# A planned order on VectorE: scans and reciprocals at their measured durations, half masks and counts at other steps

## The chip, the cores and the metric

One NeuronCore of a Trainium2 chip runs the whole program. Its engines have in-order queues of their own: TensorE (PE, with its weight loads listed as PEld), VectorE (DVE), ScalarE (ACT), GpSimd (POOL), and SyncE (SP), which issues most DMA. Engines wait for one another by semaphores. The metric is the time of one execution on the device, in microseconds (us).

## The reference, cut to what matters

A gated linear attention (4 batches, 8 heads, 768 tokens, head size 48) makes the rows of a mixture of experts with a two-level gate (3072 tokens of 384, 4 groups of 4 experts, hidden size 1024). Each token goes to one expert.

```python
for t in range(S):
    state = alpha[:, :, t, :, None] * state + np.einsum('bhd,bhe->bhde', k[:, :, t], v[:, :, t])
    y[:, :, t] = np.einsum('bhd,bhde->bhe', q[:, :, t], state)
x = np.ascontiguousarray(attn_out.transpose(0, 2, 1, 3)).reshape(B * S, H * D)
...
g_idx = np.argmax(g_logits, axis=1)
...
    e_idx = np.argmax(e_logits, axis=1)
...
        h = np.maximum(xg[mask_e] @ w1[g, e], 0.0)
        ye = h @ w2[g, e]
        out[tok_idx] = combined[:, None] * ye
```

## The kernel before

**The attention stage.** The tokens are cut into 24 chunks of 128 (6 to a batch; chunk n is step n of every series below), the 8 heads lie in 4 pairs over 112 partitions. For one chunk, in words and by the names of the plan:

- SP loads it (`load`, L463). DVE scans the gates backward (`rev`, L469, tile kd), takes the reciprocal of the end values (`turn`, L475, tile starts) and scans forward (`forth`, L480, tile cq).
- POOL multiplies the keys by kd (`key`, L485) and the queries by cq (`query`, L489).
- PE multiplies keys with queries (`score`, L503) into the two PSUM tiles zs, one for each head of a pair. There is one set of zs, so the scores of chunk n + 1 wait until both halves of chunk n are read.
- Each half is masked to the causal triangle and put into the tile sm, in one of two ways: DVE multiplies it by a mask in one step (`mask`, L512), or ACT copies it (`mask`, L517) and POOL cuts it (`cut`, L520).
- PE transposes the keys (`turn_k`, L532, into a part of the zo of the chunk before, after ACT's copy of that zo), ACT copies them (`kept`, L537), PE multiplies them with the values (`gain`, L545), DVE adds the old state (`grow`, L554, tile sums), and ACT scales the sum by kd to the new state (`scale`, L558, four for a chunk).
- PE makes the outputs from sm (L569) and adds what the old state gives (L578), in the PSUM tile zo. ACT copies zo (`copy`, L584, tile yt). PE turns yt into rows of the experts' input and gate logits (`row`, L592), which ACT keeps (L597, L609).

**Routing, by groups of chunks.** Group 0 is chunks 0 to 5, group 1 chunks 6 to 11, and so on. DVE chooses the expert of each token (from `logits`, L612, to `pick`, L673) and its weight (`weigh`). PE counts the tokens ahead of each one with small matmuls (`counts`, L773 to L781), DVE takes out the token's own count (`own`, L720) and makes its place (`place`, L727), and POOL sends each chunk's rows to these places in DRAM with one indirect DMA (`scatter`, L746). After the scatters of groups 0 and 1 SP fetches the first rows of two experts (L802), which DVE transposes (`xt`, L810).

**The experts.** From about 123 us PE multiplies the rows of all 16 experts (L281), ACT applies the relu (L297) and copies (L308), and POOL sends the results to their tokens.

**What sets the order.** Every step of the attention and routing stage is an entry of a plan: a name, an engine, an estimated duration, what it comes after. `Plan.order` (L52) is a list scheduler that runs when the program is built. It plays the plan through with the estimates, and gives each engine, whenever it comes free, the entry with the longest way still to go among those that are ready within `patience` us; `spread` adds a random number from `seed` to each entry's way. What comes out is one fixed order for each engine, and the queues of the chip follow it whatever the durations turn out to be. `BY_VECTOR[n]` says how many of the two mask halves of chunk n DVE does (the rest are ACT's and POOL's), and `COUNTED[g]` at which place in PE's hand-written series of quarter chunks the counts of group g stand.

## Time and profile before

| what | value |
|---|---|
| time, median of 3 runs | 379.44 us (378.81 to 379.56) |
| the profiled execution | 381.04 us |
| its span from the first to the last instruction | 379.2 us |
| mean granted clock of PE | 0.997 |
| busy: PE, PEld | 369.1 us (97%), 350.5 us (92%) |
| busy: DVE, ACT, POOL | 157.5 (42%), 119.5 (32%), 200.8 us (53%) |

The profiled execution's time is 1.84 us longer than its span, and 1.60 us above the median. Busy shares are over the whole span; the attention stage is its first third, and DVE and POOL have most of their work there.

### The profile page before, as it was taken

The page shows a single profiled execution, that of the slowest core. Times are in us where ns is not written, and L with a number is a line of the kernel's source. Part 1 is how long each engine was busy: PE and PEld are TensorE (multiplying, and loading weights), DVE is VectorE, ACT ScalarE, POOL GpSimd, SP SyncE. Part 2 cuts the span into 40 slices and gives each one's busy share as a digit, 9 for nine tenths or more (in the row PEclk, how much of TensorE's full clock was granted, in tenths as well). Part 3 has the DMA queues.
Part 4 walks back from the last instruction along what each step waited for, and adds up shares of the span by engine and source line. Part 5 has one row for each costly group of instructions (what it writes and reads, how often), then busy time and mean ns, then how long its engine had stood idle before and what let it go on. Part 6 is the DMA issues. An engine that isn't in the chain of part 4 may idle for free.

```text
span 379.2 us, 10153 instructions
## 1 busy us (share of the span) xinstructions
PE 369.1 (97%) x4120; PEld 350.5 (92%) x4120; DVE 157.5 (42%) x346; ACT 119.5 (32%) x315; POOL 200.8 (53%) x241
## 2 busy tenths in 40 slices
PE   7899999999999999999999999999999999999994
PEld 5788888888879999999999999999999999999983
DVE  7799899998866420238202022020220211201200
ACT  2666757866653220211112121121211212111210
POOL 6898779999876042616254261634525326236251
PEclk9999999999999999999999999999999999999998
DMA  7999997879873599999976475866769667755001
GB/s 276 397 401 399 409 402 265 267 252 338 329 240 149 165 295 346 344 352 361 339 247 217 183 244 227 285 225 209 235 238 300 218 200 247 284 199 192 8 22 37
DMA packets 30787, 98.08 MB, mean 259 GB/s; under 512 B 18040, under 2 KB 19764, under 8 KB 26131
## 3 DMA queue, kind: packets, MB, share of 16 engines
q1 hardware_dynamic: 25955, 87.87, 66.6%
q0 software_dynamic: 4784, 9.55, 7.3%
q8 instruction: 33, 0.54, 0.6%
q14 instruction: 15, 0.12, 0.1%
HBM read 85.76 MB, written 12.07 MB: 258 GB/s over the span
## 4 chain that ended last, share of the span: by engine, by line
PE 93%; DVE 2%; issue 1%; DMA 1%; ACT 1%; POOL 0%; POOLq 0%; DVEq 0%
PE bank L281 63%; PE zs L503 6%; PE zo L569 6%; PE bank L592 5%; PE zo L578 3%; PE zo L532 3%; PE bank L545 3%; PE zs L281 2%; PE bank L1359 2%; DVE kd L469 1%; DVE cq L480 1%; DMA in<-in_rows_dram 1%; PE bank L781 1%; ACT yt L584 0%; POOL in L489 0%
## 5 line engine op out<-in xcount | busy, mean ns | idle before, releaser
L1194 POOL DMA_INDIRECT out_dram<-yq,dst_q x98 | 95.4, 974 | 146.0 <-DVE yq L1190 109.6
L281 PE MATMUL bank<-hT,w 128*64 128x96 f32 (+14 forms) x768 | 117.5, 318 | 0.0
L281 PEld LDWEIGHTS bank<-hT,w 128*128 128x128 f32 (+1 forms) x768 | 115.5, 183 | 0.0
L281 PE MATMUL bank<-xt_e,w 128*64 128x120 f32 (+14 forms) x816 | 113.5, 311 | 0.0
L281 PEld LDWEIGHTS bank<-xt_e,w 128*128 128x128 f32 (+1 forms) x816 | 111.6, 178 | 0.2 <-issue 0.2
L1237 DVE SCALAR_TENSOR_TENSOR dst_q<-xq,past_q 128x7 int32<-128x7 int32 (+1 forms) x13 | 2.2, 166 | 150.5 <-DMA out_dram<-yq,dst_q 150.5
L297 ACT ACTIVATE hT<-bank 128x192 f32<-128x192 f32 (+15 forms) x68 | 32.0, 471 | 97.7 <-PE bank L281 74.8
L308 ACT COPY yT<-bank 128x192 f32<-128x192 f32 (+28 forms) x30 | 11.9, 396 | 98.5 <-PE bank L281 98.5
L746 POOL DMA_INDIRECT slots_d<-xr,place x24 | 24.1, 1006 | 6.7 <-issue 3.6
L592 PE MATMUL bank<-wr,yt 112*64 112x116 f32 x384 | 25.7, 267 | 0.3 <-ACT yt L584 0.3
L592 PEld LDWEIGHTS bank<-wr,yt 112*64 112x64 f32 x384 | 20.6, 137 | 1.0 <-ACT yt L584 0.5
L1187 DVE STREAM_TRANSPOSE yq<-yT 128x672 f32<-128x672 f32 (+2 forms) x16 | 12.6, 789 | 18.3 <-ACT yT L308 18.3
L485 POOL TENSOR_TENSOR in<-in,kd 112x512 f32<-112x512 f32 (+1 forms) x15 | 16.7, 1118 | 5.9 <-DVE kd L469 5.9
L517 ACT COPY sm<-zs 128x512 f32<-128x512 f32 x27 | 15.8, 588 | 12.2 <-PE zs L503 11.1
L558 ACT ACTIVATE state<-sums,kd 112x48 f32<-112x48 f32 x64 | 17.9, 334 | 3.0 <-DVE sums L554 2.8
L469 DVE TENSOR_TENSOR_SCAN kd<-in,starts 112x516 f32<-112x516 f32 (+1 forms) x15 | 17.0, 1140 | 4.1 <-DMA in<-in_rows_dram 3.1
L489 POOL TENSOR_TENSOR in<-in,cq 112x512 f32<-112x512 f32 (+1 forms) x16 | 16.9, 1058 | 3.4 <-DVE cq L480 3.3
L503 PE MATMUL zs<-in 48*64 48x128 f32 (+1 forms) x352 | 16.2, 274 | 2.3 <-POOL in L489 2.2
L520 POOL TENSOR_SCALAR_AFFINE_SELECT sm<-sm 128x512 f32<-128x512 f32 x27 | 17.0, 641 | 1.6 <-ACT sm L517 1.5
L480 DVE TENSOR_TENSOR_SCAN cq<-in,starts 112x516 f32<-112x516 f32 (+1 forms) x16 | 17.3, 1090 | 1.1
L503 PEld LDWEIGHTS zs<-in 48*64 48x64 f32 (+1 forms) x352 | 13.5, 148 | 4.0 <-POOL in L489 3.2
L584 ACT COPY yt<-zo 112x512 f32<-112x512 f32 x24 | 14.1, 586 | 8.5 <-PE zo L578 6.6
(161 smaller groups left out, 406.0 us busy)
## 6 DMA issues: line engine op xcount, KB each, us to landing
w<-in_w_dram SPq DMA_DIRECT2D x36, 1536.0 KB
in<-in_rows_dram SPq DMA_DIRECT2D x11, 962.5 KB
w<-in_rows_dram SPq DMA_DIRECT2D x10, 962.5 KB
xq<-slots_d SPq DMA_DIRECT2D x28, 85.8 KB
slots_d<-blank SPq DMA_DIRECT2D x2, 980.0 KB
xq<-slots_d SPq DMA_DIRECT2D x24, 73.5 KB
out_dram<-yq,dst_q POOLq DMA_INDIRECT x98
in<-in_rows_dram SPq DMA_DIRECT2D x4, 256.0 KB
```

The costliest lines, as they stand in the source:

```text
L281: nc.tensor.matmul(z[s], lhsT=w[:, s], rhs=x, start=first, stop=last, skip_group_check=True)
L297: nc.scalar.activation(out=hT[:, f0:f0 + 2, 0:n], in_=z[:, 0:2 * n].rearrange("p (f t) -> p f t", f=2), func=AF.Relu)
L469: nc.vector.tensor_tensor_scan(out=flat(c.kd[:, p0:p1])[:, ::-1], data0=c.t[0:R, A1 * p1:A1 * p0:-1], data1=one_col.to_broadcast([R, A1 * ...
L480: nc.vector.tensor_tensor_scan(out=flat(c.cq[:, p0:p1]), data0=c.t[0:R, A1 * p0:A1 * p1], data1=starts[0:R, A1 * p0:A1 * p1], initial=1.0, ...
L489: nc.gpsimd.tensor_tensor(out=c.q[:, p0:p1], in0=c.q[:, p0:p1], in1=c.cq[:, p0:p1, 1:A1], op=ALU.mult)
L503: nc.tensor.matmul(c.zs[i][s, p, :], lhsT=c.k[r, p, s], rhs=c.q[r, p, :], start=True, stop=True)
L520: nc.gpsimd.affine_select(out=c.sm[:, i], in_=c.sm[:, i], pattern=[[0, HP], [1, P]], compare_op=ALU.is_ge, fill=0.0, base=0, channel_multi ...
L558: nc.scalar.activation(out=c.st[:, p, 0:D], in_=chunks[c.n - 1].sums[:, p], func=AF.Copy, scale=c.kd[:, p, 0:1])
L569: nc.tensor.matmul(of(c.zo, p)[o], lhsT=c.v[:, h * D:h * D + o.stop - o.start], rhs=c.sm[:, i, p, :], start=(p < 2), stop=(c.bc == 0), ski ...
L592: nc.tensor.matmul(z[s, p * W:(p + 1) * W], lhsT=c.yt[:, p, s], rhs=wr[:, p, :], start=True, stop=True)
L746: sent = nc.gpsimd.indirect_dma_start(out=slots_by[t], out_offset=bass.IndirectOffsetOnAxis(ap=m["place"][:, c:c + 1], axis=0), in_=xr[:, ...
L1194: nc.gpsimd.indirect_dma_start(out=out_by.popleft().rearrange("n (j w) -> (n j) w", j=4), out_offset=bass.IndirectOffsetOnAxis(ap=dst[:, b ...
```

## The change

Five edits, all of them in what the planner is told, apart from the first, which only lets either half of chunk 0's backward scan come first:

- `back` makes its tiles at whichever half is called first.
- `BY_VECTOR`, from `[1, 0, 0, 1, 1, 2, 0, 0, 0, 1, 1, 2, 1, 1, 1, 0, 0, 2, 2, 1, 0, 2, 0, 2]` to `[1, 2, 0, 2, 1, 0, 0, 0, 2, 0, 1, 1, 2, 1, 1, 0, 0, 1, 1, 2, 0, 2, 0, 1]`. Both have the sum 21.
- `COUNTED`, from `[15, 19, 11]` to `[15, 24, 11]`: the counts of group 1 come five quarter chunks later in PE's series.
- The estimate of a backward scan of four pairs goes from 1.142 to 1.26 us, that of a reciprocal from 0.2 to 0.29.
- The planner's patience, seed and spread change.

```diff
         def back(c, p0, p1):
-            if p0 == 0:
+            if not hasattr(c, "kd"):
                 c.kd = work.tile([R, HP, A1], F32, name="kd", bufs=4)
...
-        COUNTED = [15, 19, 11]
+        COUNTED = [15, 24, 11]
...
-                add(f"rev{n}.{i}", DVE, 0.05 + 0.273 * k, partial(back, c, p0, p1),
+                add(f"rev{n}.{i}", DVE, 0.1 + 0.29 * k, partial(back, c, p0, p1),
...
-            add(f"turn{n}", DVE, 0.2, partial(turn, c, 0, HP), after=ends_of(n, "rev", c.back))
+            add(f"turn{n}", DVE, 0.29, partial(turn, c, 0, HP), after=ends_of(n, "rev", c.back))
...
-        plan.emit(patience=0.4, seed=10, spread=0.0)
+        plan.emit(patience=.2, seed=4, spread=.5)
```

The scheduler makes a new order of this. No engine gains or loses an instruction. At three places that order reads as follows; the scans are listed as SCALAR_TENSOR_TENSOR, and the numbers behind a name are those of the buffers.

**Place A, VectorE, chunks 1 to 4.** Before, from the scan of chunk 3 to the scan and sums behind it (sums_329 belong to the state that chunk 2 needs):

```order
L469 SCALAR_TENSOR_TENSOR kd_279<-in_236,starts_120 112x516
L475 RECIPROCAL starts_120<-kd_279 112x4
L480 SCALAR_TENSOR_TENSOR cq_280<-in_236,starts_120 112x516
L554 TENSOR_TENSOR sums_329<-state1_122,bank_306 112x192
L469 SCALAR_TENSOR_TENSOR kd_341<-w1_2_277,starts_120 112x516
L475 RECIPROCAL starts_120<-kd_341 112x4
L480 SCALAR_TENSOR_TENSOR cq_342<-w1_2_277,starts_120 112x516
L512 TENSOR_TENSOR sm_381<-zs0_360,causal_68 128x512
L469 SCALAR_TENSOR_TENSOR kd_396<-w2_2_327,starts_120 112x516
L554 TENSOR_TENSOR sums_420<-state0_121,bank_384 112x192
```

Now, from the second of two masks of chunk 1 (sm_262) to the sums behind the masks of chunk 3 (sums_424):

```order
L512 TENSOR_TENSOR sm_262<-zs1_230,causal_68 128x512
L469 SCALAR_TENSOR_TENSOR kd_279<-in_235,starts_120 112x516
L475 RECIPROCAL starts_120<-kd_279 112x4
L480 SCALAR_TENSOR_TENSOR cq_280<-in_235,starts_120 112x516
L469 SCALAR_TENSOR_TENSOR kd_334<-w1_2_277,starts_120 112x516
L475 RECIPROCAL starts_120<-kd_334 112x4
L554 TENSOR_TENSOR sums_357<-state1_122,bank_310 112x192
L480 SCALAR_TENSOR_TENSOR cq_335<-w1_2_277,starts_120 112x516
L469 SCALAR_TENSOR_TENSOR kd_378<-w2_2_319,starts_120 112x516
L512 TENSOR_TENSOR sm_409<-zs0_364,causal_68 128x512
L512 TENSOR_TENSOR sm_409<-zs1_365,causal_68 128x512
L554 TENSOR_TENSOR sums_424<-state0_121,bank_389 112x192
```

Two masks of chunk 1 are new ahead of the scan of chunk 3, and the first sums (now sums_357) stand behind the scan of chunk 4 and its reciprocal instead of ahead of both. The sums after these (sums_424) follow row for row: behind the two masks of chunk 3, where before they came right behind the scan of chunk 5.

**Place A, ScalarE,** which scales these sums. Before:

```order
L558 ACTIVATE state0_121<-sums_329,kd_225 112x48 x3
L584 COPY yt_370<-zo_297 112x2x2x128
L558 ACTIVATE state0_121<-sums_329,kd_225 112x48
L517 COPY sm_381<-zs1_361 128x512
L537 COPY kt_394<-zo_376 128x448
```

Now:

```order
L558 ACTIVATE state0_121<-sums_357,kd_226 112x48
L584 COPY yt_374<-zo_301 112x2x2x128
L558 ACTIVATE state0_121<-sums_357,kd_226 112x48 x3
L537 COPY kt_398<-zo_382 128x448
L597 COPY xr_88<-bank_400 128x4x96
```

The copy of yt stands behind one scale of the state (state0) instead of behind three. On POOL one cut of chunk 2 goes to between the key and the query of chunk 3; it stood behind that query.

**Place B, VectorE, chunks 11 to 14.** Before, from the masks of chunk 11:

```order
L512 TENSOR_TENSOR sm_1022<-zs0_988,causal_68 128x512
L512 TENSOR_TENSOR sm_1022<-zs1_989,causal_68 128x512
L554 TENSOR_TENSOR sums_1039<-state0_121,bank_1004 112x192
L469 SCALAR_TENSOR_TENSOR kd_1042<-w1_2_821,starts_120 112x516
L475 RECIPROCAL starts_120<-kd_1042 112x4
L480 SCALAR_TENSOR_TENSOR cq_1043<-w1_2_821,starts_120 112x516
```

Now, from the scan of chunk 14:

```order
L469 SCALAR_TENSOR_TENSOR kd_1003<-w1_2_804,starts_120 112x516
L512 TENSOR_TENSOR sm_1015<-zs0_990,causal_68 128x512
L554 TENSOR_TENSOR sums_1040<-state0_121,bank_1006 112x192
L475 RECIPROCAL starts_120<-kd_1003 112x4
L480 SCALAR_TENSOR_TENSOR cq_1004<-w1_2_804,starts_120 112x516
```

One mask of chunk 11 instead of two stands ahead of the sums, and so does the scan of chunk 14, which came behind them. On ACT three scales of these sums stand ahead of the next copy of yt, where there were two. Some rows earlier, `own` and `place` of group 0 go from right behind the scan of chunk 12 to behind its reciprocal too.

**Place C, VectorE, chunks 18 to 22.** Before, from the masks of chunk 18 to the scan of chunk 22 (kd_1693) and the logits of group 2:

```order
L512 TENSOR_TENSOR sm_1596<-zs0_1562,causal_68 128x512
L512 TENSOR_TENSOR sm_1596<-zs1_1563,causal_68 128x512
L469 SCALAR_TENSOR_TENSOR kd_1620<-w2_2_1482,starts_120 112x516
L475 RECIPROCAL starts_120<-kd_1620 112x4
L480 SCALAR_TENSOR_TENSOR cq_1621<-w2_2_1482,starts_120 112x516
L512 TENSOR_TENSOR sm_1665<-zs0_1636,causal_68 128x512
L737 SCALAR_TENSOR_TENSOR early_held_76<-seen_87,starts_120 128x2
L740 TENSOR_TENSOR seen_87<-seen_87,starts_120 128x2
L469 SCALAR_TENSOR_TENSOR kd_1693<-in_1583,starts_120 112x516
L612 TENSOR_REDUCE lg_125<-lgp_127 128x120
```

Now, over the same steps:

```order
L512 TENSOR_TENSOR sm_1576<-zs0_1547,causal_68 128x512
L469 SCALAR_TENSOR_TENSOR kd_1591<-w2_2_1491,starts_120 112x516
L720 TENSOR_TENSOR own_1613<-bank_1580,picked_85 128x96
L727 TENSOR_REDUCE place_1617<-own_1613 128x6
L475 RECIPROCAL starts_120<-kd_1591 112x4
L480 SCALAR_TENSOR_TENSOR cq_1592<-w2_2_1491,starts_120 112x516
L737 SCALAR_TENSOR_TENSOR early_held_76<-seen_87,starts_120 128x2
L740 TENSOR_TENSOR seen_87<-seen_87,starts_120 128x2
L469 SCALAR_TENSOR_TENSOR kd_1657<-in_1569,starts_120 112x516
L512 TENSOR_TENSOR sm_1687<-zs0_1633,causal_68 128x512
L512 TENSOR_TENSOR sm_1687<-zs1_1634,causal_68 128x512
```

`own` and `place` of group 1 (L720, L727), which stood before the masks of chunk 17, come in behind the scan of chunk 21, and the two masks of chunk 19 (sm_1687) behind the scan of chunk 22 (kd_1657). Before, one of these masks was ACT's and the other stood ahead of that scan. On POOL the six scatters of group 1 stood among the keys, queries and cuts of chunks 17 to 21, and now stand among those of chunks 21 and 22.

## Rows read from the trace of the kernel before

**Rows 1.** The page's totals: busy us, share of the span, instructions.

```profile
PE 369.1 (97%) x4120; PEld 350.5 (92%) x4120; DVE 157.5 (42%) x346; ACT 119.5 (32%) x315; POOL 200.8 (53%) x241
```

**Rows 2.** The chain that ended last, in order of time: start, us, what.

```profile
58.50 0.60 PE zo L532 x4
...
84.72 0.54 ACT kt L537
...
123.67 1.37 PE bank L281 x27
```

**Rows 3.** Busy us of each engine in a stretch, clock, DMA share.

```profile
55.00:60.00 5.00, 4.98 (x113) 4.38 (x111) 4.86 (x8) 3.12 (x9) 4.65 (x5) 1.00 0.67 213
```

**Rows 4.** PE's waits, 13 to 125 us: total us, times, longest.

```profile
PE bank L281 <- ACT yT L308: 0.4, 1, 0.4
PE bank L592 <- ACT yt L584: 0.3, 1, 0.3
PE zs L281 <- issue: 0.2, 1, 0.2
PE zo L569 <- ACT kt L537: 0.2, 1, 0.2
```

**Rows 5.** Timeline of DVE at place A: start, us, line, op, wait.

```profile
14.40 1.23 DVE L469 TENSOR_TENSOR_SCAN kd<-in,starts 112x516 f32<-112x516 f32 x1 [1.87 <-DMA in<-in_rows_dram]
...
17.09 0.33 DVE L554 TENSOR_TENSOR sums<-state,bank 112x192 f32<-112x192 f32 x1
17.34 1.22 DVE L469 TENSOR_TENSOR_SCAN kd<-w,starts 112x516 f32<-112x516 f32 x1
18.59 0.19 DVE L475 RECIPROCAL starts<-kd 112x4 f32<-112x4 f32 x1
...
20.61 1.22 DVE L469 TENSOR_TENSOR_SCAN kd<-w,starts 112x516 f32<-112x516 f32 x1
```

**Rows 6.** Timeline of ACT at place A.

```profile
18.53 0.59 ACT L584 COPY yt<-zo 112x512 f32<-112x512 f32 x1 [0.19 <-PE zo L578]
```

**Rows 7.** Timeline of POOL at place A.

```profile
17.26 1.18 POOL L489 TENSOR_TENSOR in<-in,cq 112x512 f32<-112x512 f32 x1 [0.36 <-DVE cq L480]
18.39 1.22 POOL L520 TENSOR_SCALAR_AFFINE_SELECT sm<-sm 128x512 f32<-128x512 f32 x2
```

**Rows 8.** Timeline of PE at place A.

```profile
19.65 0.60 PE L532 MATMUL zo<-ident,in 112*128 112x112 f32 x4
```

**Rows 9.** Timeline of DVE at place B.

```profile
56.76 0.34 DVE L554 TENSOR_TENSOR sums<-state,bank 112x192 f32<-112x192 f32 x1
```

**Rows 10.** Timeline of ACT at place B.

```profile
57.14 0.56 ACT L558 ACTIVATE state<-sums,kd 112x48 f32<-112x48 f32 x2 [0.35 <-DVE sums L554]
57.86 0.59 ACT L584 COPY yt<-zo 112x512 f32<-112x512 f32 x1 [0.16 <-PE zo L578]
```

**Rows 11.** Timeline of DVE at place C, and the first expert rows.

```profile
79.94 0.23 DVE L720 TENSOR_TENSOR own<-bank,picked 128x96 f32<-128x96 f32 x1
...
85.81 1.22 DVE L469 TENSOR_TENSOR_SCAN kd<-w,starts 112x516 f32<-112x516 f32 x1
...
88.50 0.67 DVE L512 TENSOR_TENSOR sm<-zs,causal 128x512 f32<-128x512 f32 x1
...
90.35 1.23 DVE L469 TENSOR_TENSOR_SCAN kd<-in,starts 112x516 f32<-112x516 f32 x1 [0.93 <-ACT state L558]
...
108.75 0.47 DVE L810 STREAM_TRANSPOSE xt<-rows 128x288 f32<-128x288 f32 x1
```

**Rows 12.** Timeline of PE at place C.

```profile
90.62 1.11 PE L503 MATMUL zs<-w 48*64 48x128 f32 x32
```

**Rows 13.** Timeline of POOL at place C: first and last of six scatters.

```profile
80.79 1.01 POOL L746 DMA_INDIRECT slots_d<-xr,place  x1
...
93.30 1.01 POOL L746 DMA_INDIRECT slots_d<-xr,place  x1 [0.16 <-issue]
```

**Rows 14.** Timeline of SP: the early experts' fetch.

```profile
101.48 4.86 SPq L802 DMA_DIRECT2D rows<-slots_d  x8
```

More of the change, by code (lines that the diff above doesn't have):

```diff
@@ L792, in gla_then_hierarchical_moe @@
         WARM = (25, 5)
-        BY_VECTOR = [1, 0, 0, 1, 1, 2, 0, 0, 0, 1, 1, 2, 1, 1, 1, 0, 0, 2, 2, 1, 0, 2, 0, 2]
-        COUNTED = [15, 19, 11]
+        BY_VECTOR = [1, 2, 0, 2, 1, 0, 0, 0, 2, 0, 1, 1, 2, 1, 1, 0, 0, 1, 1, 2, 0, 2, 0, 1]
+        COUNTED = [15, 24, 11]
         LAST = 'c3 h0 row22 own h1 c4 h2 h3 h4 row23 h5 h6 h7 y0 c5 y1 y2 y3'.split()
```

## The prediction

> **What bounds the kernel now.** I read the page's totals first: PE is busy for 369.1 of 379.2 us [rows 1]. Busy matmuls are no proof, so next comes the chain that ended last. Its last piece of this kind begins at 123.67 us and is the expert part, PE alone, with each matmul behind the one before [rows 2]; nothing that this change moves is used there, except that it starts earlier or later. So the question is when PE gets to 123.67 us. Before that the chain lies on PE too, but on a PE that is fed just in time: it steps to PE's transposes at 58.50, which start right as a copy on ACT ends, to a copy on ACT at 84.72, and back [rows 2]. The table by stretches shows why: between 55 and 60 us PE is busy for 4.98 of 5 us, but DVE for 4.86 and POOL for 4.65 [rows 3]. These engines are full at once, so a place in DVE's queue is worth its time wherever PE is just behind. Last I read PE's waits: those beside the start are 0.4, 0.3, 0.2 and 0.2 us, 1.1 in all [rows 4]. That is all that a better order can win in this stage; a worse one has no such bound.
>
> **What the change costs nothing for.** Not one instruction is added or removed on any engine (DVE has 361 rows in both orders), and the sum of BY_VECTOR is 21 in both, so no work goes between engines: 21 of 48 mask halves stay on DVE. The new durations, seed, spread and patience exist in the planner alone. The change is only an order. The two scans of chunk 0 swap their halves at the start; the first scores come later by one half scan, but the second score waits for a mask that does not move, and I cost that at nothing. Moving own0 and place0 behind one reciprocal (0.19 us [rows 5]) I cost at nothing too: the rows that they place are not fetched before 101.48 [rows 14], and that distance hides it; without the cover it would be 0.2 us.
>
> **Place A, chunks 1 to 4.** DVE stood idle for 1.87 us before the scan at 14.40, waiting for a load [rows 5]. The two masks of chunk 1 go into that hole; a mask takes 0.67 us [rows 11], so two are hidden. But ahead of the state's sums, which were at 17.09, now stand the scan of chunk 4 and its reciprocal. The scan starts at 17.09 instead, takes from there to the reciprocal 1.25 us (17.34 to 18.59), and the reciprocal 0.19 [rows 5]: the sums start at about 18.55, 1.45 us later. On ACT the scales of the state stand ahead of the copy of yt. Before, three of them lay between the sums and the copy at 18.53 [rows 6]; now one does. From sums to the first scale takes 0.4 (56.76 to 57.14 is 0.38 [rows 9, 10]), one scale some 0.25 (the two at 57.14 take 0.56 [rows 10]), so the copy runs from 19.2 to 19.8, at 0.59 [rows 6]. PE's transposes of chunk 3 overwrite what it reads, and stood at 19.65 [rows 8]: late by 0.15 to 0.2. On POOL one cut (1.22 for two, 0.61 each) now stands ahead of the query at 17.26, which had 0.36 us of idle time before it [rows 7]: 0.25 later, and the scores of chunk 3 with it. Both delays fall on the same transposes, so they count once: **+0.25**.
>
> The next sums have the same fate: two masks of chunk 3 ahead of them where before none stood between the scan and the sums. The scan of chunk 5 may start earlier (20.0 instead of 20.61), if its load is there; the trace shows no wait before 20.61 [rows 5], and so not when it landed. If it is there, the two masks cost nothing more, since PE is late by 0.25 already; if it lands at 20.6, sums, scales and copy are 0.6 later, of which PE feels about 0.4. I take the middle: **+0.2** (ends: 0 and 0.4).
>
> **Place B, chunks 11 to 14.** Before, two masks, the sums at 56.76 [rows 9], then the scan of chunk 14. Now that scan and one mask stand ahead of the sums. The next instruction starts some 0.08 us before the listed end of the one ahead (17.09 + 0.33 against 17.34 [rows 5]), so a scan of 1.22 holds the queue for 1.14 and a mask for 0.6. Sums at 56.76 + 1.14 - 0.6 = 57.3, the first scale at 57.68. Three scales instead of two come ahead of the copy (0.56 and another 0.23 [rows 10]), which moves from 57.86 to about 58.4. PE's transposes started at 58.50, right on that copy's end (57.86 + 0.59 = 58.45) [rows 2, 10]: no slack at all. **+0.55**, from 0.3 (if PE is late from place A and DVE is not) to 0.9.
>
> **Place C, chunks 17 to 22.** The counts of group 1 come five steps later on PE, so own1 goes from 79.94 to behind the scan of chunk 21 at 85.81 [rows 11]. Three things follow.
>
> First, the six scatters, 80.79 to 93.30 at 1.01 us each [rows 13], leave the middle of POOL's queue and start some 6 us later; the keys and queries between them come forward. That can win the small waits of PE from 84.72 on [rows 2, 4]; I book 0.2 of the 1.1, the wait for kt, since the others are for copies on ACT, which gets no less work.
>
> Second, the scan of chunk 22, which waited 0.93 us until 90.35, now stands ahead of both masks of chunk 19. The mask before it stood at 88.50 [rows 11]. PE's scores of chunk 20 (90.62 [rows 12]) overwrite what these masks read. The point that decides: the scan must start by 90.62 - 2 x 0.6 - 1.14 = 88.3. The wait is marked as one for ACT, but the instruction named had ended long before; what ended was the chunk's load. If it lands at 90.35 again, the masks end at 92.7 and the scores are 2.1 late. Ends: 0 and 2.1. I take 0: the scatters at 80.79 to 93.30 [rows 13], which move data in the time ahead of 90.35, have then left it for the most part, and DVE comes to the scan early.
>
> By the Trainium skill's page "DMA: Bandwidth & Descriptors" (Queues, rings and completion order) each DMA engine takes turns between its queues, a packet at a time, so a load beside scatters is stretched and one without them is not. By that rule the load would be on time and this term 0; by the row's 0.93 alone, with the landing kept, it would be 2.1. No row here shows the landing by itself.
>
> Third, the last of these scatters moves from 93.30 by about 5 us (six of them now lie among five keys, queries and cuts of 1.2 and 0.6 us). The fetch of the early experts' rows at 101.48 waits for it, and issues for 4.86 us, to 106.34; their transpose is at 108.75 [rows 14, 11]. So 2.4 us of the 5 are covered, some more if expert 0 needs only the first half of the fetch (another 2.4): 0.2 to 2.6 late, while PE itself is 0.8 late by then. I take **+0.25** of net delay (ends: 0 and 1.8).
>
> **Sum.** 0.25 + 0.2 + 0.55 - 0.2 + 0.25 = +1.05 us. The profiled execution took 381.04 us (span 379.2 and 1.84 around it), 1.60 above the median of the runs, 379.44; the sum makes it 382.1, and the median **380.5**.
>
> **Rivals.**
> - *Absorbed.* All 1.1 us of PE's waits that lie behind places A and B [rows 4] shrink as PE comes later: +1.05 - 0.9 (the 1.1 without the 0.2 already booked) = +0.15, 379.6. For it: an engine that is late finds its helpers ready. Against it: DVE and POOL at 4.86 and 4.65 of 5 [rows 3] have little time to get ahead. The Trainium skill's "Perfetto Trace Analysis" (Identifying the Most-Contended Engine) judges PE by its weight loads and not by its matmuls' busy time. By the row of 55 to 60 us PEld is at 4.38 of 5 [rows 3], which would leave 0.6 us in each 5 to catch up, and the whole delay would be gone by 70 us: 379.4. The chain, which runs matmul to matmul, speaks against such room.
> - *Faster.* The scatters' 6 x 1.01 us leave POOL's fullest stretch, the load of chunk 22 is early, and the 1.1 us of waits go; places A and B cost nothing because DVE, having spent its 1.87 us of idle time on masks, is ahead by more than I count: 379.44 - 1.1 + 0.25 = 378.6. It decides at 57.86: if that copy starts no later against PE's transposes, the order has won. For it: the filled hole. Against it: 1.45 us of delay at 17.09, worked out row by row.
> - *Late masks.* The load of chunk 22 keeps its time, 2.1 on top: 382.6. Or the late fetch takes its full 1.8 in place of 0.25: 382.05.
> - *No new order where it matters* is excluded by the listing of the queues.
>
> **Numbers.** Forecast (380.0 to 381.6) 0.42; late masks or fetch 0.16; absorbed 0.23; faster 0.19. What a measurement tells from no change is 0.2%, 0.76 us: 378.7 to 380.2. Of the forecast's 0.42 some 0.03 falls below 380.2, which the tail of absorbed above it makes up. So slower 0.58, same 0.23, faster 0.19. The range of 8 in 10 reaches to the late masks at the top (382.7) and below the win of 378.6 at the bottom (378.3); it leaves out 0.10 below and 0.06 above. It has both signs, so the forecast's own range stands here: 380.0 to 381.6.
>
> **What the profile after would show.** Right: no long idle time of DVE before the scan of chunk 3; the sums of chunk 1 at 18.4 to 18.7; PE's transposes of chunk 3 at 19.8 to 20.0 and those near 58.50 at 59.2 to 59.7 with a wait for ACT's yt; first scatter of group 1 at 86 to 88; the last long PE piece at about 124.7. Wrong: transposes at 58.50 or earlier (faster), a PE wait of 2 us near 91 for masks, or a wait of DVE's xt transpose for its rows.

## The result, and the profile after

| | before | after |
|---|---|---|
| median | 379.44 us (378.81 to 380.14, 5 runs) | 382.89 us (381.78 to 384.14, 5 runs) |
| profiled execution | 381.04 us | 383.06 us |

The change makes the kernel slower: ratio 1.0091 [1.0064, 1.0118], +3.45 us by medians. The forecast was 380.5 us, with a range of 380.0 to 381.6 around it and a range of 8 in 10 of 378.3 to 382.7; the measured median lies above both. The two profiled executions differ by 2.02 us only, because that of before took 1.60 us more than its median. So costs are taken from medians, and the traces tell where they arise.

The page of after: the span and the totals (busy us, share of the span, instructions).

```profile
span 381.4 us, 10149 instructions
...
PE 368.7 (97%) x4120; PEld 351.0 (92%) x4120; DVE 157.2 (41%) x346; ACT 120.0 (31%) x315; POOL 200.7 (53%) x241
```

By the totals nothing has changed: PE is busy for 368.7 us instead of 369.1 [rows 1]. The expert part has the same length too. The chain, in order of time, at its last long piece:

```profile
125.79 239.53 PE bank L281 x1728
```

It takes 239.53 us in both traces and begins at 125.79 instead of 123.67 [rows 2], 2.12 later. All of it was lost before. The table by stretches shows in which stage PE had no work; first before, then after (stretch, its length, busy us and instructions of PE, PEld, DVE, ACT, POOL, granted clock, DMA share, GB/s).

```profile
13.00:60.00 47.00, 46.47 (x871) 40.20 (x867) 43.10 (x71) 32.73 (x94) 39.30 (x50) 1.00 0.99 385
60.00:80.00 20.00, 20.00 (x464) 17.44 (x463) 18.63 (x35) 14.75 (x43) 19.18 (x21) 1.00 0.82 276
80.00:100.00 20.00, 19.76 (x437) 17.07 (x439) 18.25 (x40) 12.07 (x35) 17.71 (x18) 1.00 0.92 338
100.00:120.00 20.00, 19.43 (x417) 16.93 (x408) 12.82 (x55) 10.39 (x34) 15.77 (x30) 1.00 0.66 223
```

```profile
13.00:60.00 47.00, 46.47 (x877) 40.23 (x876) 43.27 (x72) 32.83 (x95) 38.07 (x48) 1.00 0.98 382
60.00:80.00 20.00, 18.93 (x422) 16.60 (x420) 17.30 (x33) 13.90 (x39) 19.02 (x20) 1.00 0.82 280
80.00:100.00 20.00, 20.00 (x462) 17.64 (x463) 19.11 (x40) 13.41 (x41) 17.06 (x19) 1.00 0.82 305
100.00:120.00 20.00, 17.68 (x391) 15.74 (x388) 11.61 (x48) 10.93 (x32) 16.25 (x19) 1.00 0.70 237
```

Length less PE's busy time gives its idle time: 0.53, 0, 0.24 and 0.57 us before; 0.53, 1.07, 0 and 2.32 after. The new stops are in two stages. PE's own rows of after have each of them (start, us, line, operation, and in brackets the idle time ahead and what ended it):

```profile
20.40 0.60 PE L532 MATMUL zo<-ident,in 112*128 112x112 f32 x4
...
25.23 0.60 PE L532 MATMUL zo<-ident,w 112*128 112x112 f32 x4 [0.27 <-ACT yt L584]
...
51.24 0.60 PE L532 MATMUL zo<-ident,in 112*128 112x112 f32 x4
...
59.80 0.60 PE L532 MATMUL zo<-ident,in 112*128 112x112 f32 x4 [0.24 <-ACT yt L584]
...
77.18 0.60 PE L532 MATMUL zo<-ident,in 112*128 112x112 f32 x4 [1.07 <-ACT yt L584]
...
92.37 1.11 PE L503 MATMUL zs<-w 48*64 48x128 f32 x32
...
103.02 0.89 PE L503 MATMUL zs<-in 48*64 48x128 f32 x24 [0.85 <-issue]
...
112.99 0.72 PE L281 MATMUL zs<-xt,w 128*64 128x96 f32 x12 [1.47 <-DVE sums_e L690]
```

The four rows of transposes (L532) at the top answer to these of before, and to 19.65 and 58.50 [rows 2, 8]:

```profile
24.15 0.60 PE L532 MATMUL zo<-ident,w 112*128 112x112 f32 x4
...
50.16 0.60 PE L532 MATMUL zo<-ident,in 112*128 112x112 f32 x4
```

So PE is 0.75 us late at chunk 3's transposes (19.65 to 20.40), 1.08 late at the next (24.15 to 25.23), still 1.08 late at 51.24, and 1.30 late behind place B (58.50 to 59.80). The 0.75 is older than place A: it comes from the first 13 us. Then PE waits 1.07 at 77.18, stops 0.85 in the scores of chunk 22 at 103.02, and waits 1.47 at 112.99 for expert 0. Before has stops of its own in the same stretch (0.2 and 0.3 us at expert 0's first product and right behind it [rows 4]), and some slower groups of matmuls, so that only 2.12 us remain between the two traces at the experts.

What stands behind the wait at 77.18 are these rows of DVE and ACT in after:

```profile
70.50 1.23 DVE L469 TENSOR_TENSOR_SCAN kd<-in,starts 112x516 f32<-112x516 f32 x1 [1.42 <-DMA in<-in_rows_dram]
...
73.58 1.23 DVE L469 TENSOR_TENSOR_SCAN kd<-in,starts 112x516 f32<-112x516 f32 x1 [0.29 <-DMA in<-in_rows_dram]
74.72 0.33 DVE L554 TENSOR_TENSOR sums<-state,bank 112x192 f32<-112x192 f32 x1
...
76.51 0.29 DVE L658 TENSOR_REDUCE starts<-lg 128x30 f32<-128x120 f32 x1
...
76.55 0.58 ACT L584 COPY yt<-zo 112x512 f32<-112x512 f32 x1
```

DVE waits 1.42 and 0.29 us for the loads of chunks 17 and 18, and the state's sums that stand behind both backward scans come at 74.72. ACT scales, copies yt at 76.55, and PE starts as that copy ends. The same rows of DVE before:

```profile
70.39 1.22 DVE L469 TENSOR_TENSOR_SCAN kd<-in,starts 112x516 f32<-112x516 f32 x1
...
73.08 0.33 DVE L554 TENSOR_TENSOR sums<-state,bank 112x192 f32<-112x192 f32 x1
73.33 1.22 DVE L469 TENSOR_TENSOR_SCAN kd<-in,starts 112x516 f32<-112x516 f32 x1
```

The scan of chunk 17 starts at nearly the same time in both (70.39 and 70.50). So the wait of 1.42 us by itself makes nothing late: it is the room in which the choice of group 1 stood, whose first row is now at 76.51. The sums are 1.64 us later because the scan of chunk 18, with its wait of 0.29, now stands ahead of them instead of behind them.

And behind the wait at 112.99: the first and the last scatter of group 1 on POOL, the fetch on SP, and DVE's transpose of the fetched rows.

```profile
89.10 1.01 POOL L746 DMA_INDIRECT slots_d<-xr,place  x1
...
99.93 1.01 POOL L746 DMA_INDIRECT slots_d<-xr,place  x1 [0.16 <-issue]
...
107.34 4.73 SPq L802 DMA_DIRECT2D rows<-slots_d  x8
...
112.37 0.48 DVE L810 STREAM_TRANSPOSE xt<-rows 128x288 f32<-128x288 f32 x1 [2.48 <-DMA rows<-slots_d]
```

The first scatter went from 80.79 to 89.10, the last from 93.30 to 99.93 [rows 13], the fetch from 101.48 to 107.34 [rows 14], the transpose from 108.75 [rows 11] to 112.37, where DVE itself waits 2.48 us for the rows. The row of PE at 112.99 names the instruction of DVE right behind the transpose; what the product reads is the transpose, which ends at 112.85. PE's last counts ahead of it, in before and in after:

```profile
109.24 0.41 PE L781 MATMUL bank<-seen,ident 128*128 128x64 f32 x2
...
111.11 0.41 PE L781 MATMUL bank<-seen,ident 128*128 128x64 f32 x2
```

### The profile page after: what moved, and what is told of

Read it like the earlier page. It is cut to its first block, busy times and chain, and to the rows that moved or that the text cites. A ratio compares the mean times of both kernels' runs of the same rounds, so it can differ in the third digit from the quotient of the medians.

```text
span 381.4 us, 10149 instructions
## 1 busy us (share of the span) xinstructions
PE 368.7 (97%) x4120; PEld 351.0 (92%) x4120; DVE 157.2 (41%) x346; ACT 120.0 (31%) x315; POOL 200.7 (53%) x241
## 4 chain that ended last, share of the span: by engine, by line
PE 74%; DMA 9%; DVE 7%; issue 4%; POOL 2%; ACT 2%; SPq 1%; POOLq 0%; DVEq 0%
PE bank L281 63%; DMA w<-in_rows_dram 3%; DMA in<-in_rows_dram 3%; DVE kd L469 2%; PE zs L281 2%; PE bank L1359 2%; PE bank L592 2%; DVE sm L512 2%; PE zo L569 1%; PE zs L503 1%; DMA slots_d<-xr,place 1%; DVE cq L480 1%; PE zo L578 1%; DMA rows<-slots_d 1%; POOL slots_d L746 1%
## 5 line engine op out<-in xcount | busy, mean ns | idle before, releaser
L281 PE MATMUL bank<-hT,w 128*64 128x96 f32 (+14 forms) x768 | 117.5, 318 | 0.0
L281 PEld LDWEIGHTS bank<-hT,w 128*128 128x128 f32 (+1 forms) x768 | 115.4, 183 | 0.0
L281 PE MATMUL bank<-xt_e,w 128*64 128x120 f32 (+14 forms) x816 | 113.5, 311 | 0.0
L281 PEld LDWEIGHTS bank<-xt_e,w 128*128 128x128 f32 (+1 forms) x816 | 111.6, 178 | 0.2 <-issue 0.2
```

The lines of the kernel that those rows point to most:

```text
L281: nc.tensor.matmul(z[s], lhsT=w[:, s], rhs=x, start=first, stop=last, skip_group_check=True)
```

## The experiments

All kernels compute the whole reference. A "share" is the kernel's time over that of the kernel before, run beside it on the same chip, with a 95% interval. It is not the quotient of the two medians, and lies up to 0.2% off it (e5: 0.50% against 0.34% by medians). Differences of shares are taken against the 0.91% of the change. For the single moves, a list takes entries of the plan out of their engine's order and puts them behind another entry of that engine; nothing else in the order changes. In the plan's names `grow` is L554, `hidden0.0` expert 0's first matmuls (L281), `xt0` its transpose, `from23` what the state gives to the last chunk's outputs (L578), `place3` the places of group 3, `max1` to `pick1` the choice of group 1, and `forth`, `rev`, `key`, `query`, `cut` and `scatter` are as told above, with the chunk's number.

**One part back, or one part alone.** *Counts back, rest of the change kept:*

```diff
-        COUNTED = [15, 24, 11]
+        COUNTED = [15, 19, 11]
```

> The changed kernel with the counts of group 1 back at their old step (COUNTED 19 instead of 24), all else as changed. In the order this puts the choice of group 1 ahead of the scan of chunk 17 again and the six scatters some 5 us earlier. Theory 1 (the later counts cost most: choice and sums wait behind loads near 70 us, scatters, fetch and first expert rows come late near 110): gives back 1.5 to 2.2 of the 3.45 us, 380.7 to 381.4. Theory 2 (the front of the program costs most: the start's swapped halves and the later sums at places A and B): gives back under 0.5, 382.4 or more.

380.40 us, share 1.0025 [1.0007, 1.0044]: 2.5 of the 3.45 us are gone (0.66%, from 0.3 to 1.0 by the two intervals), and what is left is near the limit of the measurement. The later counts are the main cause, with the caveat that the planner makes another order for them in other places too. *Counts alone,* the reverse edit in the kernel before:

> The kernel before with nothing changed but the counts of group 1 five steps later (COUNTED 24). Theory 1: slower by 1.0 to 2.2 us, 380.4 to 381.6, with PE waiting for xt near 110 us. Theory 2: within 0.4 us of the kernel before.

381.50 us, 1.0050 [1.0032, 1.0068]. The fetch starts at 104.18, and PE has the wait of after near 77 us, as 0.72 at 75.72. But against the expectation it does not wait for expert 0: the rows are transposed at 108.48, ahead of PE's need at 110.97. In their place stand waits for POOL, 0.39 and 0.28 us for queries at 100.89 and 105.68 and 0.61 for a cut at 109.34. So the late counts cost in both orders, but in part by other ways. The whole change costs 0.41% more than they do alone, which is clear of the intervals (0.1 to 0.7); whether e1 took away more than the 0.50 is not, at 0.66. *Mask halves alone:*

```diff
-        BY_VECTOR = [1, 0, 0, 1, 1, 2, 0, 0, 0, 1, 1, 2, 1, 1, 1, 0, 0, 2, 2, 1, 0, 2, 0, 2]
+        BY_VECTOR = [1, 2, 0, 2, 1, 0, 0, 0, 2, 0, 1, 1, 2, 1, 1, 0, 0, 1, 1, 2, 0, 2, 0, 1]
```

> The kernel before with only the new BY_VECTOR. Its order has the two masks of chunk 1 in DVE's idle time, the sums at place A ahead of the scan of chunk 4 as before, and those at place B one mask earlier. If the masks' placing alone is a gain: 378.3 to 378.9. If the masks that go to ACT and POOL elsewhere cost as much: 379.2 within 0.4. If the halves carry a part of the loss: 379.8 or more.

379.66 us, 0.9998 [0.9979, 1.0016]: nothing. *Patience, seed and spread alone:*

```diff
-        plan.emit(patience=0.4, seed=10, spread=0.0)
+        plan.emit(patience=.2, seed=4, spread=.5)
```

> The kernel before with only the new patience, seed and spread. It starts with the swapped halves of chunk 0, and own and place of group 0 stand late. If the start costs in its own right: 379.7 to 380.2 (0.5 to 1.0 slower). If the start is made up later: 379.2 within 0.4.

383.16 us, 1.0108 [1.0082, 1.0134]: as slow as the whole change, but by another order. Its PE waits 1.11 at 46.66 for a yt, with sums that stand behind a scan and the logits. The parts do not add up (0.50, 0 and 1.08% against 0.91%), since each makes a new order everywhere. Moving single rows tells more.

**The start.** *Chunk 0's halves in the old order, rest kept:*

```diff
+        swap = {"rev0.0": "rev0.1", "key0.0": "key0.1", "forth0.0": "forth0.1", "query0.0": "query0.1"}
+        swap.update({b: a for a, b in swap.items()})
+        done = [swap.get(n, n) for n in done]
```

> The changed kernel with the two halves of chunk 0 in the old order (scan, key, forward scan and query of the first half first). Theory 2: the 0.75 us that PE is late after chunk 2 go and stay gone to the end: 382.1. Theory 1: PE is earlier by 0.75 us up to 70 us, but the waits near 75 and 110 us do not move with it, and the time gets back 0.3 us or less: 382.6 to 382.9.

382.43 us, 1.0082 [1.0051, 1.0112]. The 0.46 us is inside the intervals; in its trace PE instead waits 0.82 at 19.63 for POOL's query, and is no earlier at the next transposes (25.41). *The kernel before once more:*

> The kernel before, for a second profile of it, since its first profiled execution was 1.6 us above its median. Theory 1: the waits of this second profile in 84 to 124 us are smaller than in the first, and PE comes to the expert part up to 1.3 us before 123.67. Theory 2: it comes there at 123.67 within 0.3 us, and the difference lies in the expert part or outside the span.

380.44 us; PE reaches the experts at 123.17 with a stop of 1.10 at 96.28. The kernel before has no such stop there in its first profile. So stops of about 1 us come and go from one execution of the same kernel to the next.

**The fetch.** *Expert 0's matmuls and its transpose later, rest kept:*

```diff
+MOVES = [(['hidden0.0'], 'from23'), (['xt0'], 'place3')]
```

> The changed kernel with two moves near 110 us: PE's first product for expert 0 comes behind the outputs of the last chunk, and DVE's first xt transpose behind place 3, so that nothing waits for the late fetch at 112.4. Theory 1a (the late scatters cost by way of the fetch of the first expert rows; PE idle for 1.47 us there): gives back 1.0 to 1.5 us, 381.4 to 381.9. Theory 1b (the late counts cost by other ways, the choice and sums near 70 us and traffic at 90 to 107): gives back under 0.4, 382.5 or more.

381.06 us, 1.0050 [1.0032, 1.0068]: 0.41% less than after, 1.6 us, by the intervals 0.3 to 2.8. The other versions of the changed kernel agree: e3 above and e6, e9 and e10 below leave expert 0 in its place and are at 0.82 to 0.95%, e11 moves it too and is at 0.41. PE's idle time between 100 and 120 us falls from 2.32 to 0.24. *The same move in the kernel before,* where the fetch is early:

> Control for e5: the kernel before with the same two moves near 110 us. If e5 gained because of the late fetch alone: within 0.4 us of the kernel before, since there the fetch is in time. If the later place of expert 0's first product is better in itself: 378.0 to 378.8, and e5's 1.6 us are in part not the fetch's.

379.47 us, 1.0005 [0.9991, 1.0019]. The move itself gives nothing, so what e5 gains is what the late fetch costs.

**The choice and the sums.** *Choice early, with ACT's exp:* `max1` to `pick1` and `exp1` go behind `grow13`.

> The changed kernel with the choice of group 1 (max to pick, and the exp) back ahead of the scan of chunk 17 on DVE, as in the kernel before; counts, scatters and all else as changed. Theory 1b: the choice then fills the 1.42 us in which DVE waits for a load at 70.5, PE's wait of 1.07 us at 77.2 goes, and 0.4 to 1.0 us come back: 381.9 to 382.5. Theory 1a: 0.2 us or less, 382.7 or more.

382.55 us, 1.0090 [1.0066, 1.0114]. No gain. The scan of chunk 17 now starts without a wait, but PE still waits 0.69 for yt at 76.41, with the sums behind the scan of chunk 18. And ACT stood 1.24 us idle until 69.13 for the input of exp1, which was moved with the others, so this run doesn't decide what the choice costs. *Sums ahead of the second scan:* `grow14` behind `forth17`.

> The changed kernel with one instruction moved on DVE: the sums that follow the forward scan of chunk 17 go ahead of the scan of chunk 18, as before, instead of behind it. Theory 3 (sums that stand behind a scan that waits for a load are a cost of their own): PE's wait of 1.07 us for ACT's copy at 77.2 goes and 0.6 to 1.1 us come back, 381.8 to 382.3. Theory 1a (only the late fetch counts, since PE has to wait at 112 for it anyway): 0.2 us or less, 382.7 or more.

382.83 us, 1.0083 [1.0053, 1.0113]. The wait of 1.07 is gone:

```profile
75.27 0.60 PE L532 MATMUL zo<-ident,in 112*128 112x112 f32 x4
...
77.69 1.09 PE L569 MATMUL zo<-sm,w 128*48 128x128 f32 x16 [0.41 <-POOL in L489]
```

So it is the place of the sums, not that of the choice, that makes the wait. A wait of 0.41 for POOL's query stands right behind, and the time is 0.3 us better, well inside the intervals. *Choice without exp1, and sums:*

```diff
+MOVES = [(['max1', 'less1', 'first1', 'best1', 'group1', 'one1', 'pick1'], 'grow13'), (['grow14'], 'forth17.0')]
```

> The changed kernel with DVE's order of chunks 16 to 18 as before: the choice of group 1 ahead of the scan of chunk 17, and the sums that follow ahead of the scan of chunk 18 (unlike e6, ACT's order is left alone). Theory 1a (the fetch is a barrier at a fixed time): PE's wait near 77 us goes, but what it wins is lost again in the wait for xt near 112 us, and 0.4 us or less come back: 382.5 or more. Theory 6 (waits add up): 0.9 to 1.2 us come back, 381.7 to 382.0.

*The same and e5's moves:*

> The same with the moves of e5, so that nothing waits for the late fetch. Theory 1a: the two together give 2.4 to 2.8 us back, 380.1 to 380.5, since the win at 77 us is now kept. If it is 381.1 or more, the wait near 77 us costs nothing of its own, and 1.7 us of the loss stay unexplained by these two places.

These two ran on a third chip, where the kernel before too was slower (382.08), so only the shares compare: 1.0054 [1.0027, 1.0081] and 1.0061 [1.0033, 1.0089] (384.10 and 384.43 us). e17 alone would be worth 1.4 us against after, with an interval that takes in 0, but with e5's moves nothing is added to it, nor it to them. In its trace PE is so late that it no longer waits for expert 0's transpose, only 1.03 us for a yt behind it. By these runs the place of the choice and the sums costs between 0 and 1.4 us.

**Places A and B.** *Sums back ahead of the scans:* `grow1` behind `forth3`, `grow2` behind `rev5`, `grow10` behind `forth13`.

> The changed kernel with three instructions moved on DVE: the sums at place A ahead of the scan of chunk 4 and right behind that of chunk 5, those at place B ahead of the scan of chunk 14, as before. Theory 3: 0.3 to 0.8 us come back, 382.1 to 382.6. Theory 1a: PE is earlier by that much up to 70 us, but the fetch near 107 us does not move, so 0.2 us or less, 382.7 or more.

383.29 us, 1.0095 [1.0066, 1.0123]: no gain. *All moves (e5, e9, e10):*

> The changed kernel with the moves of e5, e9 and e10 together: nothing waits for the late fetch, and the four sums stand where they stood before. Theory 3 with 1a: 1.6 us from the fetch, 0.9 from the sums at chunk 17, 0.4 from places A and B: 379.8 to 380.3, of which the rest to 379.3 is not explained. If the sums cost nothing beside the fetch: 381.0 within 0.3.

381.47 us, 1.0041 [1.0018, 1.0063], no better than e5 alone.

**The scatters by themselves.** *In the kernel before, only POOL's six scatters of group 1 moved to where after has them:*

```diff
+MOVES = [(['scatter6'], 'key21.0'), (['scatter7'], 'query21.0'), (['scatter8'], 'cut0.20'),
+         (['scatter9'], 'cut1.20'), (['scatter10'], 'key22.0'), (['scatter11'], 'query22.0')]
```

> The kernel before with only POOL's order changed: the six scatters of group 1 wait until the key of chunk 21 and lie between the operations of chunks 21 and 22, as in the changed kernel; counts, choice, own and place stay early. Theory 4 (where the scatters stand is the cause, with the fetch behind them, whatever the counts do): 381.0 to 381.8, and PE waits for xt near 111 us. Theory 5 (the counts themselves cost, by the choice and places that come late): within 0.4 us of the kernel before.

383.14 us, 1.0093 [1.0071, 1.0116]: one queue's rows cost as much as the whole change. But not at the fetch. PE's rows, and the table by stretches behind them:

```profile
101.30 1.11 PE L503 MATMUL zs<-in 48*64 48x128 f32 x32 [1.14 <-POOL in L489]
...
107.35 1.21 PE L503 MATMUL zs<-in 48*64 48x128 f32 x32 [1.54 <-POOL in L489]
...
109.32 1.77 PE L592 MATMUL bank<-wr,yt 112*64 112x116 f32 x15
...
108.00:110.00 2.00, 2.00 (x46) 1.83 (x37) 1.16 (x4) 0.00 (x0) 1.81 (x3) 0.65 0.67 179
110.00:112.00 2.00, 2.00 (x24) 2.00 (x22) 1.85 (x8) 1.49 (x5) 1.82 (x3) 0.50 0.66 193
```

The scatters stand ahead of the queries of chunks 22 and 23, PE waits 1.14 and 1.54 us for these, and behind the second of these waits its granted clock is 0.65 and 0.50 for 4 us: the 15 matmuls at 109.32 take 1.77 us, where such a group takes 0.97 at a clock of 1.00 (at 103.37 in the same trace). Behind the first the clock stays at 1.00. *With e14's moves added,* to take the fetch out:

> The kernel before with the late scatters of e13 and the moves of e14. Theory 4 with the fetch as its only way: back at the time of e14. If the crowd of twelve scatters on POOL and the DMA queues at 88 to 112 us costs beside the fetch: 0.8 to 1.5 us above e14.

383.57 us, 1.0098 [1.0074, 1.0123], with the same waits and the same low clock. By PE's rows the queries are the cause here, and the fetch is hidden behind them. In after PE waits for no query between 13 and 125 us, so this is not its way.

**Looking for a better order.** *Mask halves, and the counts of group 2 later:* the edit of e7, and `counts2` behind `turn_k21` on PE.

> The kernel of e7 (before, with only the new BY_VECTOR) with the counts of group 2 moved on PE from ahead of the scores of chunk 21 to behind that chunk's transposes, since PE waited there for the picks (0.58 us in e7, 1.10 in the second profile of before). If that wait is a cost: 379.1 to 379.4, faster than e7 and the kernel before by 0.3 to 0.6. If the later places and scatters take it back: 379.7 or more.

379.71 us, 1.0020 [0.9991, 1.0049]: no gain. *e1, with `grow1` and `grow2` as in e10:*

> The kernel of e1 (changed, counts back at 19) with the sums at place A ahead of the scan of chunk 4 and right behind that of chunk 5. If the rest of e1's loss (0.25%) lies in place A: 379.4 to 379.8. If not: 380.4 within 0.4.

380.50 us, 1.0031 [1.0016, 1.0046]: what e1 has left does not lie in place A. No version beats the kernel before; e7, e12 and e14 equal it within what can be measured.

## Why the prediction was wrong, step by step

The direction was right and the size too small. Booked were 1.05 us; 3.45 came.

**The step that failed: the fetch, booked at +0.25.** Its chain was right: scatters late, fetch late, transpose late. Its size was not, above all the cover. I let 2.4 us of the lateness be covered, and another 2.4 if expert 0 needs only half of the fetch, and left out the time from the issue to the landing. In after the rows are there 5.03 us behind the start of the fetch (107.34 to 112.37). An estimate: by the same time they were there at 106.5 in before, 2.2 us ahead of their transpose at 108.75, and that was the whole cover. The last scatter also came 6.63 us later and the fetch 5.86, where I had counted 5. So the transpose came 3.62 us later (108.75 to 112.37). PE itself was 1.87 late at the counts ahead of it (109.24 to 111.11), where I had counted 0.8; 1.75 are left. The wait in the trace is 1.47, since in before the transpose was done somewhat ahead of PE's first product. That DVE's transpose waits for its rows, by 2.48 us, was one of the prediction's own signs of being wrong. e5 with its control e14 gives 1.6 us for the whole term, near its upper end of 1.8, though with a wide interval. With that dear end the sum would have been 1.05 - 0.25 + 1.8 = 2.6 us.

**A step that was missing: the choice and the sums near 70 us.** I followed the late counts into `own`, the scatters and the masks, but not into what the planner puts in the room that they leave. The choice of group 1 went behind two scans, the sums behind one scan more than before, as at places A and B, and PE waits 1.07. e2 has the wait with the counts alone, so they are what moves these rows, and e9 shows that it is the sums. The wait is shown. The pair of traces below puts its cost at about 1.1 us, but no move won that back (e9, e17, e18).

**The start, booked at nothing.** In the trace of after it is not nothing. The table by stretches:

```profile
6.00:8.00 2.00, 0.38 (x6) 0.26 (x6) 1.59 (x2) 0.00 (x0) 1.31 (x2) 1.00 0.99 331
8.00:10.00 2.00, 2.00 (x22) 1.70 (x21) 1.93 (x5) 0.63 (x2) 1.75 (x2) 0.67 1.03 412
10.00:12.00 2.00, 2.00 (x15) 1.47 (x15) 1.86 (x4) 0.49 (x1) 1.79 (x4) 0.50 1.07 434
...
6.00:8.00 2.00, 1.16 (x16) 1.04 (x16) 1.93 (x5) 0.00 (x0) 1.52 (x3) 1.00 1.00 343
8.00:10.00 2.00, 1.34 (x15) 0.93 (x12) 2.00 (x4) 1.03 (x2) 2.00 (x3) 1.00 0.99 390
10.00:12.00 2.00, 2.00 (x35) 1.74 (x36) 1.86 (x3) 0.90 (x2) 1.80 (x3) 1.00 1.09 449
```

The upper three are of after, the lower three of before. In after the first scores start at 7.74 instead of 6.84, PE has 0.38 us of work between 6 and 8 us, and its granted clock is 0.67 and 0.50 in the next two stretches; in before it has 1.16, and the clock stays at 1.00. That is the 0.75 us at chunk 3. It is no fixed price: of 11 profiled executions with the swapped start three show it, of the nine with the old start none, and e16, with 0.42 us of work there, keeps 1.00. The eight without the fall come to the transposes of chunk 3 at 19.59 to 20.15, the old start with the old order there (eight more) at 19.61 to 20.11. By these rows the swap costs by the clock or not at all, and e3 gained no more than its interval. What it costs on average was not settled.

**Places A and B, +0.45 and +0.55: right places, too dear by what the runs show.** The rows of after:

```profile
19.11 0.34 DVE L554 TENSOR_TENSOR sums<-state,bank 112x192 f32<-112x192 f32 x1
...
21.22 1.23 DVE L469 TENSOR_TENSOR_SCAN kd<-w,starts 112x516 f32<-112x516 f32 x1 [0.63 <-DMA w<-in_rows_dram]
...
19.73 0.57 ACT L584 COPY yt<-zo 112x512 f32<-112x512 f32 x1
...
59.18 0.56 ACT L584 COPY yt<-zo 112x512 f32<-112x512 f32 x1
```

Beside the 0.75 from the start PE loses 0.33 at A, with a wait of 0.27 for yt at 25.23; the load of chunk 5 was late, as the dear end had it (a wait of 0.63 at 21.22). This is no clean price, since the start hides a part of it: the copy at 19.73 ends at 20.30, 0.65 after 19.65, and PE comes only at 20.40. Other executions help. With the new order at A and no fall of the clock at the start five come to the transposes of chunk 4 at 24.42 to 24.90 (e5, e6, e9, e17, e18), with the old order six at 24.15 to 24.65 (before, e2, e4, e13, e14, e15): some 0.2 us apart in the mean, and hardly to be told apart. (e3, which waits 0.82 for a query, is left out.) At B PE loses 0.22 instead of 0.55, although ACT's copy comes 1.32 us after 57.86, because PE was already 1.08 late. e10 shows that putting the sums back gives nothing. **The 0.2 given back by earlier keys** can't be told: between 80 and 100 us after has no idle time, 0.24 less than before, but the kernel before has 1.16 there in e4, and e14, with the same order up to there, none. e1, with the old counts, has 1.14.

**The late masks, booked at 0 with an end of 2.1: right.**

```profile
89.73 1.23 DVE L469 TENSOR_TENSOR_SCAN kd<-in,starts 112x516 f32<-112x516 f32 x1
90.88 1.26 DVE L512 TENSOR_TENSOR sm<-zs,causal 128x512 f32<-128x512 f32 x2
```

The scan of chunk 22 starts at 89.73 with no wait, the masks at 90.88, and PE's scores at 92.37 wait for nothing. The rule quoted from the Trainium skill's "DMA: Bandwidth & Descriptors" (Queues, rings and completion order) agrees with this row: without scatters ahead of it, the load was in time. But the rows do not prove it: e12 and e14 have the scatters as early as before, and there this scan starts at 88.68 and 89.35 with no wait either, while e4 waits 1.84.

**The rival "absorbed" falls.** The table by stretches of after, where PE's lateness of 1.08 us at 25.23 would have had time to go:

```profile
26.00:40.00 14.00, 14.00 (x273) 12.32 (x270) 13.24 (x21) 10.11 (x29) 13.35 (x16) 1.00 1.04 392
40.00:50.00 10.00, 10.00 (x188) 8.62 (x184) 9.07 (x22) 7.54 (x25) 5.94 (x7) 1.00 1.02 421
```

PEld is at 12.32 of 14 and 8.62 of 10, which by the reading of the Trainium skill's "Perfetto Trace Analysis" (Identifying the Most-Contended Engine) would leave some 3 us to catch up, an estimate; PE's matmuls are at 14.00 and 10.00, and it is 1.08 late at 51.24 as at 25.23. The way from the transposes of 24.15 to those of 50.16 takes 26.01 us in before, in after, and in e1, which is 2.08 us late on it. The trace does not bear that reading out here: the matmul stream, not the weight loads, is what is full. **"Faster"** fell by its own test, the copy at 57.86, which now stands at 59.18, more than PE's delay.

**The base.** I summed against a profiled execution with 1.34 us of idle time of PE between 13 and 120 us and took its excess over the median off as a constant. Stops like these come and go (e4), and after's were added to a base that already held some.

**What is left behind e5's moves, and what stays open.** e5 has 0.50% (1.9 us) left. Its trace and that of e14, in which expert 0 is moved too and PE waits for no fetch either, show where: e5 comes to the experts 1.57 us later (123.12 and 121.55), and the execution is 1.61 us longer (380.53 and 378.92). It is 0.12 us late at the transposes of chunk 4 (24.42 and 24.30), 0.55 behind place B (59.11 and 58.56), and 1.66 at the transposes of chunk 19 (89.12 and 87.46), after this wait:

```profile
76.74 0.60 PE L532 MATMUL zo<-ident,in 112*128 112x112 f32 x4 [1.31 <-ACT yt L584]
```

Behind that nothing is added. So in this pair the rest is place B and the sums near 77 us. These are single executions, and moving the sums did not lower the time: other waits came in their place, 0.41 for a query in e9 and 0.96 for the kept keys at 79.33 in e11. Whether any order wins the 1.9 us back stays open. The stop at 103.02, where eight matmuls into the scores of chunk 22 PE stands for 0.85 us and waits for nothing that the profile shows, is unexplained too. At the same place e8 stops for 0.66, e17 for 0.79, e16 for 0.39, e18 for 0.29, e6 for 0.22 and before for 0.06 (though its scores took 1.45 us in all, not 1.11). The traces of e5 and e11 have no such stop, and no experiment singles it out.

## What to carry to other kernels

When a planner moves one step, read what it puts into the room that comes free, and above all which short row now stands behind one long row more (the sums behind the scan of chunk 18), and what waits for the last of a series of scatters: these are behind the waits of 1.07 and 1.47 us, while the full stretches of DVE at places A and B cost 0.2 to 0.3. A wait that only fills room which another row had filled, as that of 1.42 us, makes nothing late by itself. A transfer that waits for the last of a series costs its lateness less the cover, which ends where the data land and not where the issue ends, and less what the bound engine is late itself; measure that by moving its consumer in both kernels (e5 and e14), not from one trace. Compare idle time stage by stage and row by row, and take differences of 1 us from medians, since one execution can hold that much of its own.

## What the hardware showed that was not expected

A wait of PE can cost more than its length. The clearest is e13 above; here is e10, behind a wait of 1.61 us for expert 0 at 113.03:

```profile
112.00:114.00 2.00, 0.97 (x12) 1.00 (x14) 1.42 (x8) 0.04 (x1) 0.98 (x1) 0.76 0.79 235
114.00:116.00 2.00, 2.00 (x25) 2.00 (x23) 0.32 (x2) 0.13 (x1) 1.26 (x2) 0.50 0.84 167
116.00:118.00 2.00, 2.00 (x41) 1.64 (x40) 1.76 (x9) 0.71 (x2) 1.95 (x3) 0.89 0.93 381
```

PE is idle for 1.03 us of the first stretch, and the granted clock is 0.76 there, then 0.50 (1.2 of 2.4 GHz), then 0.89. The work between 114 and 116 us is 25 matmuls in place of 45 in after. But it does not follow from a wait's length alone: after waits 1.47 at the same place, and its clock stays at 1.00 there. e10's order differs from that of after by three sums only, so a wait of about the same length can cost a microsecond more in one execution than in another. That may be part of why single traces and medians differ; no run here shows how much.
